# A fused attention, gated MLP and SoLU layer on one Trainium2 core: block 0's up products 512 tokens wide, x in the buffers of p

## Chip, core and metric

The kernel runs on one core of one Trainium2 chip. The metric is the device time of one execution in microseconds (us); the median of three runs of the kernel before is 970.23 us. Engines are called by the names of the profile: PE (TensorE, with PEld its weight loads), DVE (VectorE), ACT (ScalarE), POOL (GpSimd) and SP (SyncE, which here issues most DMAs). SPq is SP's sequencer.

## What is computed

Chunked attention with 8 memory keys a head, then two feed-forward layers on the 3072 tokens of 512 features that it yields:

```python
for c in range(24):                      # chunks of 32 tokens, keys c*32-16 .. c*32+40
    scores = scale * q_c @ concat(mem_k, k_ctx).T
    a = exp(scores - max); a = a / (sum(a) + 1e-9)
    out[c] = a @ concat(mem_v, v_ctx)
x = heads side by side                   # 3072 x 512
h = sigmoid(x @ w_gate) * (x @ w_val)    # 3072 x 1536
y = h @ w_out                            # 3072 x 512
z = y @ w_in                             # 3072 x 1024
s = z * softmax(z)
out = ((s - mean) / sqrt(var + 1e-6) * g_ln) @ w2_out
```

The weights come as 64-bit floats and are converted on the chip: a piece of 512 KB yields 128 x 512 values.

## The kernel before

The tokens are 24 tiles of 128. For tile t, the attention turns k and q on PE (`d_k`, `d_q`, four 128x128 transposes each, L446), takes the scores (`d_scores`, 64 small matmuls, L505), their maximum and exponential (`a_max`, `a_exp`, tile s), turns p (`d_p`), multiplies with v (`d_pv`), normalises (`d_norm`, tile xs) and turns the result (`d_x`), which ACT and DVE split into xh (`a_xhi`, L600) and xl (`a_xlo`, L604). The scores of tile t need the first keys of tile t + 1. p is the exponential in place: tile s holds both. The pool sp has two buffers of s and two of xs.

Four tiles are a block j of 512 tokens. For each of 12 groups m of 128 hidden features, `up` (L609 to L620) makes two products, one with the gate weights (gv = 0) and one with the val weights (gv = 1): 12 matmuls each, (wh, xh), (wh, xl) and (wl, xh) over four slices of the 512 features. `up_sig` (ACT) and `up_mul` (DVE) make g, which `g_store` writes to HBM; it is read again for `down`. In blocks 1 to 5 a matmul takes all 512 columns. In block 0, `steps_of` gives 256 tokens at a time: m = 0 to 10 for tiles 0 and 1, then m = 0 to 10 for tiles 2 and 3, then m = 11 for all four. A pair of products therefore needs only two tiles' x, but each weight passes PE twice.

A weight piece (m, gv) is loaded on SP's queue (`w_load`, L408), converted by ACT (`w_exp`, L204) and DVE (`w_bits`, L209 to L215), split by ACT (`w_hi`, L269) and POOL (`w_lo`, L220). The raw pieces share three buffers r and three larger spare places.

The order of all engines' work is made by the class `Plan`: each step has an engine, an assumed duration, steps it depends on, buffers it takes (`acq`, counted against the capacities given to `Plan`) and gives back (`rel`), and a due time, which is handed back from a step to those ahead of it. `order` puts the steps on their engines, the one due first among those that could start; no step is put more than AHEAD = 40 before it is due. The due times of the up products are a running clock from FIRST = 30, and x is due one unit before its block's first product that uses it, and LEAD earlier still in blocks 1 to 5. On the chip each engine executes its steps in the order so made, and waits with everything behind a step for that step.

Of the kernel before, what the change touches and what calls it, by code (L numbers as in the profile page):

```python
# [9 lines left out]
F32 = mybir.dt.float32  # L10
# [11 lines left out]
class Plan:  # L22
# [9 lines left out]
    def add(self, name, eng, dur, fn=None, deps=(), due=None, acq=(), rel=(), dma=(), table=None, prev=None, pad=0,  # L32
            slack=0):


        self.tasks[name] = dict(
            name=name, eng=eng, dur=dur, fn=fn, deps=list(deps), due=due, acq=list(acq), rel=list(rel),
            dma=dma, table=table, pad=pad, slack=slack, end=None, next=[], prev=prev if prev in self.tasks else None,
        )
# [84 lines left out]
def encoder_kernel(  # L124
# [16 lines left out]
    B, H, S, D = q.shape  # L141
# [10 lines left out]
    MF = FF // 128  # L152
# [75 lines left out]
    for m in range(MF):  # L228
        pieces.append((m, 0, w_out.bitcast(I32)[m * 128:(m + 1) * 128, :].unsqueeze(1)))
        if m < 2 * KM:  # L230
            kk, n = divmod(m, 2)
# [179 lines left out]
    at = ExitStack()  # L411
    raw = at.enter_context(tc.tile_pool(name="raw", bufs=2))
    tp = at.enter_context(tc.tile_pool(name="tp", bufs=2))
    ktp = at.enter_context(tc.tile_pool(name="ktp", bufs=3))
    sp = at.enter_context(tc.tile_pool(name="sp", bufs=2))
    sm = at.enter_context(tc.tile_pool(name="sm", bufs=2))

    R, QT, KT, VW, SS, PT, PS, RS, XS, X = ({} for _ in range(10))
# [39 lines left out]
    def d_load(nm, t):  # L458
        b, i = divmod(t, TB)
        R[nm, t] = raw.tile([128, H, D], F32, tag=nm, name=nm)  # L460
        src = dict(rk=k, rq=q)[nm][b, :, i * 128:(i + 1) * 128, :]
        nc.sync.dma_start(out=R[nm, t], in_=src.rearrange("h p d -> p h d"))
# [61 lines left out]
        nc.scalar.activation(out=SS[t], in_=SS[t], func=AF.Exp, scale=D ** -0.5)  # L524

    def a_sum(t):
        rs = RS[t] = sm.tile([128, H], F32, tag="rs", name="rs")
        nc.vector.tensor_reduce(out=rs, in_=SS[t], axis=AX.X, op=ALU.add)
        nc.vector.tensor_single_scalar(out=rs, in_=rs, scalar=1e-9, op=ALU.add)
        nc.vector.reciprocal(out=rs, in_=rs)  # L530
# [49 lines left out]
        PS[t, 2] = two_banks(PT[t], VW[t // 2][:, :, 4 * (t % 2):4 * (t % 2) + 4, :])  # L580

    def d_norm(t):
        XS[t] = sp.tile([128, H, D], F32, tag="xs", name="xs")
        rs = RS.pop(t).unsqueeze(2).to_broadcast([128, H, D]).rearrange("p (k x) d -> p x k d", x=2)
        out_ = XS[t].rearrange("p (k x) d -> p x k d", x=2)
        nc.vector.tensor_tensor(out=out_, in0=PS.pop((t, 2)), in1=rs, op=ALU.mult)
        SS.pop(t)

    def d_x(t):
        PS["dx", t] = d_turn("u0", XS.pop(t))  # L590
# [275 lines left out]
    def o_store(j, t):  # L866
# [2 lines left out]


    plan = Plan(dict(
        rk=2, rq=2, qT=2, pT=2, kT=3, vw=2, s=2, xs=2,
        a=2, P=1, Q=1, R=1, O=1, hs0=1, hs1=1, hu=1, y=1, ys=1, xh=2, xl=2, r=3, w=2, u0=2, u1=2, sg=2, g=2, gh=3, gl=3, so=2, nt=6, e=1, hi=2, lo=2, o=2,
        **{s: 1 for s in FIRST_TAGS},
    ))
    add = plan.add
    ACT, DVE, POOL, PE, SP = "act", "dve", "pool", "pe", "sp"
    HALVES, WIDE = 1, 1
    FIRST, RATE, LEAD, SLACK, EARLY, LATER = 30.0, 1.12, 20.0, 3.0, 140.0, 235.0

    ALONE = "c2", "nt", "gcol", "mhalf", "ident", "zero", "pb"

    def one(nm, t, eng, dur, fn, deps=(), **kw):
        add((nm, t), eng, dur, lambda: fn(t), deps=[d if isinstance(d, tuple) or d in ALONE else (d, t) for d in deps],
            prev=(nm, t - 1), **kw)
# [17 lines left out]
    for t in range(NTILE):  # L903
        n, u = divmod(t, 2)
        b, i = divmod(t, TB)
        early = t < 2
        one("rk", t, SP, 0.1, lambda t: d_load("rk", t), acq=[("rk", t)], dma=[1.456])
        one("dk", t, PE, 0.9 if early else 0.5, d_k, ["ident", "rk"], acq=[("u0", ("dk", t)), ("kT", t)], rel=[("rk", t)], slack=0 if t < 6 else SLACK)
        one("dkev", t, ACT, 1.35, d_kev, ["dk"], rel=[("u0", ("dk", t))])
        one("dhalo", t, POOL, 0.6, d_halo, ["dkev"] + ([("dhalo", t - 1)] if i else []))  # L910
        one("dkmem", t, POOL, 0.45, d_kmem, ["dkev", ("dmev", b)])
        one("rq", t, SP, 0.1, lambda t: d_load("rq", t), acq=[("rq", t)], dma=[1.456])
        one("dq", t, PE, 0.9 if early else 0.5, d_q, ["ident", "rq"], acq=[("u1", ("dq", t)), ("qT", t)], rel=[("rq", t)], slack=0 if t < 6 else SLACK)
        one("dqev", t, ACT, 0.58, d_qev, ["dq"], rel=[("u1", ("dq", t))])
        one("sw", t, PE, 1.3 if early else 0.75, d_scores,
            ["dqev", "dkmem", ("dhalo", t if i == TB - 1 else t + 1)],
            acq=[("a", t), ("s", t)], rel=[("qT", t), ("kT", t)], slack=0 if t < 6 else SLACK)
        one("max", t, DVE, 1.45, a_max, ["sw"], rel=[("a", t)])
        one("exp", t, ACT, 0.63, a_exp, ["max"], table="exp")
        one("sum", t, DVE, 1.25, a_sum, ["exp"])  # L920
        one("dp", t, PE, 0.9 if early else 0.5, d_p, ["exp"], acq=[("u1", ("dp", t)), ("pT", t)], slack=0 if t < 6 else SLACK)
        one("dpev", t, ACT, 0.58, d_pev, ["dp"], rel=[("u1", ("dp", t))])
        one("pv", t, PE, 1.3 if early else 0.75, d_pv, ["dpev", ("dv", n, 0), ("dv", n, 1), ("dvm", n)],
            acq=[("a", (t, 2)), ("xs", t)], rel=[("pT", t)] + ([("vw", n)] if u else []), slack=0 if t < 6 else SLACK)
        one("norm", t, DVE, 0.69, d_norm, ["pv", "sum"], rel=[("a", (t, 2)), ("s", t)])
        x = [("xh", t // 4), ("xl", t // 4)] if t % 4 == 0 else []
        one("dx", t, PE, 0.9 if early else 0.5, d_x, ["norm"], acq=[("u0", ("dx", t))] + x, rel=[("xs", t)], slack=0 if t < 6 else SLACK)
        one("xhi", t, ACT, 0.58, a_xhi, ["dx"] + ([] if t % 4 == 0 else [("xhi", t - 1)]))
        one("xlo", t, DVE, 0.69, a_xlo, ["xhi"], rel=[("u0", ("dx", t))])

# [1 line left out]

    def steps_of(j):

        if j >= HALVES:
            return [(m, (0, 512)) for m in range(MF)]
        wide = WIDE if j == 0 else 0
        return [(m, w) for w in ((0, 256), (256, 512)) for m in range(MF - wide)] + [
            (m, (0, 512)) for m in range(MF - wide, MF)
        ]  # L940

    for n, (m, gv, _) in enumerate(pieces):
        s, x = divmod(n - 3, 2)
# [3 lines left out]
        rel = [] if spare and not x else [key]  # L947
# [49 lines left out]
    clock = FIRST  # L997
    for j in range(NB):
        steps = steps_of(j)
        seen = set()  # L1000
        for s, (m, w) in enumerate(steps):
# [6 lines left out]
            for gv in range(2):  # L1008
# [6 lines left out]
                elif s == len(steps) - 1:  # L1015
# [3 lines left out]
                    rel=[("xh", j), ("xl", j)] if gv and s == len(steps) - 1 else [])  # L1019
            add(("sig", *key), ACT, 0.6 if full else 0.39, lambda k=key: up_sig(*k), deps=[("up", j, m, 0, w)],  # L1020
                acq=[("sg", key)], rel=[("u0", key)], table="sig", due=clock + 1)
# [8 lines left out]
    for m in range(MF):  # L1030
        one("gag", m, SP, 0.1, g_again, [("gst", 0, m, w) for y, w in steps_of(0) if y == m], acq=[("r", ("g", m))], dma=[0.73])
        add(("gmax", 0, m), DVE, 0.75, lambda m=m: g_max0(m), deps=[("gag", m)], rel=[("r", ("g", m))], due=EARLY + 4 + 8.0 * m)
# [12 lines left out]
    for j in range(NB):  # L1045
# [3 lines left out]
        for f in range(MF):  # L1049
            parts = [w for m, w in steps_of(j) if m == f]  # L1050
            tag, after = ("g", "sg")[f % 2], [("sig" if f % 2 else "mul", NB - 1, MF - 1, (0, 512))]
            if not f % 2:
                after.append(("gmax", NB - 1, MF - 1))
            if (j, f) in FIRST_G:
                tag, after = FIRST_G[j, f], ["c2"]
# [6 lines left out]
                acq=([(f"u{o % 2}", ("y", j, o)) for o in range(KM)] if j else [("a", ("y", o)) for o in range(2)]) if f == 0 else [], rel=[("gh", (j, f)), ("gl", (j, f))])  # L1062
        for o in range(KM):
            two("ycp", j, o, ACT, 0.62, y_copy, [("down", j, MF - 1)] + ([("ycp", j, 0)] if o else [("up", NB - 1, 11, 1, (0, 512))]),
                acq=[("y", j)] if o == 0 else [],
                rel=[(f"u{o % 2}", ("y", j, o))] if j else [("a", ("y", o // 2))] if o % 2 else [])
        if j == 0:
            add("pb", "mark", 0, open_pb, deps=[("ycp", 0, o) for o in range(KM)])
        for c in range(4):
            two("ysum", j, c, DVE, 0.72, y_sum, [("ycp", j, o) for o in range(KM)] + ([("ysum", j, c - 1)] if c else [("thi", x) for x in range(3, 7)] + [("tlo", x) for x in range(3, 7)]),  # L1070
                acq=[("ys", j)] if c == 0 else [])
            need = [("ycp", j, o) for o in range(KM)] + [("ysum", j, x) for x in ((), (), (0, 1), (2, 3))[c]]
            two("yhi", j, c, ACT, (1.15, 0.62, 1.15, 1.15)[c], y_hi, need + ([("yhi", j, 0)] if c else []),
                acq=[("xh", ("y", j)), ("xl", ("y", j))] if c == 0 else [])
            two("ylo", j, c, DVE, (1.35, 0.72, 1.35, 1.35)[c], y_lo, ["yhi"], rel=[("y", j), ("ys", j)] if c == 3 else [])
        for u in range(2):
            before = ("prod", j, 0, 3) if u else ("prod", j - 1, 1, 3)
            held = {3: [("hpart", j, u, "c22")], 2: [("hpart", j, u, "c1")], 7: [("hpart", j, u, "u2")], 4: [("hpart", j, u, "u3")]}
            for x in ORDER:
# [4 lines left out]
                    acq=[(bank, (j, u))] if x in (1, 6, 5) else [], rel=[("xh", ("y", j)), ("xl", ("y", j))] if u and x == 3 else [])  # L1084
# [3 lines left out]
            for part, (eng, need) in parts.items():  # L1088
                add(("hpart", j, u, part), eng, 0.62 if eng == ACT else 0.72, lambda j=j, u=u, p=part: h_part(j, u, p),
                    deps=[("prod", j, u, n) if isinstance(n, int) else ("hpart", j, u, n) for n in need] + ["w2done"],  # L1090
                    acq=[(f"hs{u}", (j, u)), ("hu", (j, u))] if part == "c1" else [],
                    rel={"c11": [("P", (j, u))], "c21": [("Q", (j, u))], "c12": [("R", (j, u)), ("hu", (j, u))]}.get(part, []))
        for t in range(4):
            u, x = TILE[t] % 2, TILE[t] // 2
# [3 lines left out]
                rel=[("e", (j, t, 1))] + ([(f"hs{u}", (j, u))] if x else []))  # L1098
# [10 lines left out]
                acq=[(OUT.get((j, t), "O"), (j, t))], rel=[("nt", (j, t))])  # L1109
# [3 lines left out]
    for p in range(2 * NB):  # L1113
        j, u = divmod(p, 2)
        m = [("prod", j, u, x) for x in ORDER]
# [51 lines left out]
```

## Time and profile before

| | |
|---|---|
| median of three runs | 970.23 us (969.41 to 971.39) |
| the profiled execution | 970.33 us |
| its span | 968.6 us |
| mean granted clock of TensorE | 0.989 |
| PE busy | 924.2 us (95%) |
| DVE busy | 613.7 us |
| ACT busy | 434.7 us |
| POOL busy | 91.3 us |

All times within the execution are counted from the start of the span. The busy time of PE counts matmuls, whose records overlap one another: the distance between the starts of two of them tells more of the pace than their durations. [...]

### The profile page before, as it was taken

The numbers are of one execution on the slowest core, as the hardware profiler recorded it, in microseconds if no ns is written. First come the engines' busy times: TensorE is split into PE (matmuls) and PEld (weight loads), VectorE is DVE, ScalarE is ACT, GpSimd is POOL, SyncE is SP. The second block draws the span as 40 slices with busy tenths as digits, with TensorE's granted clock in tenths as the row PEclk, the third lists the DMA queues.
The fourth block names the chain that finished last, engine by engine and source line by source line (L and its number), as shares of the span: only waits on it lengthen the run. The fifth ranks groups of instructions, "written<-read, shape, count | busy, mean of one in ns | idle before, by whom it ended". The sixth has DMA issues, their size and how long they took to land.

```text
span 968.6 us, 18485 instructions
## 1 busy us (share of the span) xinstructions
PE 924.2 (95%) x7408; PEld 614.5 (63%) x7408; DVE 613.7 (63%) x1156; ACT 434.7 (45%) x705; POOL 91.3 (9%) x154
## 2 busy tenths in 40 slices
PE   3777989999999999999999999999999999999998
PEld 2667888878888888788788644444444444444443
DVE  5787553377657757747745336786765764867581
ACT  4566542145245435326514243644544633645452
POOL 3343200001000000000003300000000000000000
PEclk9988989999999999999999999999999999999999
DMA  8999895367648746732575232434244144242323
GB/s 203 234 242 205 203 205 169 103 177 169 192 134 173 193 128 172 180 146 99 165 256 189 76 98 66 120 86 100 66 98 109 55 109 98 77 98 44 77 65 98
DMA packets 202949, 132.68 MB, mean 137 GB/s; under 512 B 153136, under 2 KB 170288, under 8 KB 202672
## 3 DMA queue, kind: packets, MB, share of 16 engines
q1 hardware_dynamic: 192624, 105.29, 43.9%
q10 hardware_dynamic: 10240, 26.22, 8.9%
q8 instruction: 58, 0.95, 0.4%
q14 instruction: 27, 0.22, 0.1%
HBM read 86.38 MB, written 33.03 MB: 123 GB/s over the span
## 4 chain that ended last, share of the span: by engine, by line
PE 89%; DMA 4%; ACT 3%; DVE 2%; SPq 2%; issue 1%; ACTq 0%; DVEq 0%
PE u L619 39%; PE y L711 19%; PE ps L856 13%; PE Q L764 5%; PE tr L446 4%; PE ps L505 3%; PE R L764 3%; PE P L764 3%; DMA r<-in_moe_w_gate_dram 1%; DMA r<-in_moe_w_val_dram 1%; SPq L569 1%; DMA vw<-mv 1%; DMA rq<-in_q_dram 1%; DVE w L210 0%; ACT L524 0%
## 5 line engine op out<-in xcount | busy, mean ns | idle before, releaser
L619 PE MATMUL u<-xh,wa 128*128 128x512 f32 (+1 forms) x1328 | 386.7, 371 | 3.7 <-ACT wa L269 1.4
L619 PEld LDWEIGHTS u<-xh,wa 128*128 128x128 f32 x1328 | 245.2, 194 | 44.5 <-ACT wa L269 1.7
L619 PE MATMUL u<-xl,wa 128*128 128x512 f32 (+1 forms) x664 | 243.7, 367 | 0.6 <-DVE xl L604 0.5
L711 PE MATMUL y<-gh,pl 128*128 128x512 f16 x576 | 176.0, 379 | 0.0
L711 PEld LDWEIGHTS <-pl 128*128 128x128 f16 x864 | 84.5, 98 | 102.0 <-issue 0.5
L619 PEld LDWEIGHTS u<-xl,wa 128*128 128x128 f32 x664 | 129.1, 194 | 19.3 <-DVE xl L604 1.5
L630 DVE TENSOR_TENSOR g<-sg,u 128x512 f32<-128x512 f32 (+1 forms) x83 | 51.1, 615 | 127.7 <-PE u L619 56.3
L856 PE MATMUL ps<-wo,nt 128*128 128x512 f16 x576 | 127.6, 379 | 0.8 <-ACT o L863 0.8
L625 ACT ACTIVATE sg<-u 128x512 f32<-128x512 f32 (+1 forms) x83 | 44.9, 542 | 160.1 <-PE u L619 117.1
L711 PE MATMUL y<-gl,pl 128*128 128x512 f16 x288 | 109.2, 379 | 0.0
L432 ACT ACTIVATE gh<-gi,gm 128x512 f16<-128x512 f32 x72 | 51.5, 719 | 127.1 <-PE y L711 121.1
L856 PEld LDWEIGHTS <-nt 128*128 128x128 f16 x576 | 56.2, 98 | 69.2 <-issue 1.3
L222 DVE SCALAR_TENSOR_TENSOR gl<-gi,gm,gh 128x512 f16<-128x512 f32 x72 | 53.7, 750 | 66.3 <-ACT gh L432 66.0
L764 PEld LDWEIGHTS <-yh 128*128 128x128 f16 x336 | 32.9, 98 | 39.7
L824 POOL TENSOR_TENSOR ls<-ls,mhalf 128x1 f32<-128x1 f32 x24 | 14.6, 611 | 370.8 <-DVE ls L820 332.4
L204 ACT ACTIVATE w<-r 128x512 f32<-128x512 f32 x46 | 30.7, 669 | 27.1 <-DMA r<-in_moe_w_gate_dram 8.6
L764 PE MATMUL Q<-pl,yh 128*128 128x512 f16 x144 | 42.8, 379 | 0.0
L281 DVE TENSOR_REDUCE gm<-g 128x1 f32<-128x512 f32 x60 | 41.0, 684 | 1.8
L785 DVE TENSOR_TENSOR pl<-Q,pl 128x512 f32<-128x512 f32 x36 | 24.8, 688 | 25.7 <-PE Q L764 25.3
L220 POOL TENSOR_TENSOR wa<-w,wa 128x512 fp32r<-128x512 f32 x24 | 34.1, 1425 | 59.1 <-ACT wa L269 57.4
L213 DVE SCALAR_TENSOR_TENSOR w<-r,w 128x512 int32<-128x512 int32 x46 | 38.6, 839 | 1.6
L797 ACT ACTIVATE e<-pl,ls,few 128x1024 f32<-128x1024 f32 x24 | 29.7, 1237 | 18.0 <-DVE ls L806 10.0
(126 smaller groups left out, 1106.5 us busy)
## 6 DMA issues: line engine op xcount, KB each, us to landing
gi<-gd SPq DMA_DIRECT2D x72, 256.0 KB
gd<-g SPq DMA_DIRECT2D x61, 256.0 KB
r<-in_moe_w_out_dram ACTq DMA_DIRECT2D x28, 512.0 KB
vw<-in_v_dram SPq DMA_DIRECT2D x64, 98.0 KB
rk<-in_k_dram SPq DMA_DIRECT2D x24, 256.0 KB
rq<-in_q_dram SPq DMA_DIRECT2D x24, 256.0 KB
out_dram<-o SPq DMA_DIRECT2D x24, 256.0 KB
wd<-r SPq DMA_DIRECT2D x20, 256.0 KB
```

Source lines behind the costliest of these rows:

```text
L213: nc.vector.scalar_tensor_tensor(out=d, in0=hi, scalar=-(2 ** 31), in1=d, op0=ALU.bitwise_and, op1=ALU.bitwise_or)
L220: nc.gpsimd.tensor_tensor(out=dst, in0=x, in1=hi, op=ALU.subtract)
L222: nc.vector.scalar_tensor_tensor(out=dst, in0=x, scalar=s, in1=hi, op0=ALU.mult, op1=ALU.subtract)
L281: nc.vector.tensor_reduce(out=dst, in_=a, axis=AX.X, op=ALU.max, apply_absolute_value=True)
L432: nc.scalar.activation(out=dst, in_=x, func=AF.Copy, scale=s)
L446: nc.tensor.transpose(pv[:, kk, :], src[:, 2 * kk:2 * kk + 2, :], ident[0:rows, 0:rows])
L619: nc.tensor.matmul(u, lhsT=a, rhs=c[:, kk, w[0]:w[1]], start=(n == 0), stop=(n == 3 * KM - 1))
L625: nc.scalar.activation(out=sg, in_=U.pop((j, m, 0, w)), func=AF.Sigmoid)
L630: nc.vector.tensor_tensor(out=g, in0=U.pop((j, m, "s", w)), in1=U.pop((j, m, 1, w)), op=ALU.mult)
L711: nc.tensor.matmul(y, lhsT=a, rhs=c, start=(f == 0 and n == 0), stop=(f == MF - 1 and n == 2))
L764: nc.tensor.matmul(ps, lhsT=yc[a][:, c, kk, u * 128:(u + 1) * 128], rhs=t[:, hl, kk, :], start=(first and n == 0), stop=(n == 5), skip_gro ...
L856: nc.tensor.matmul(ps, lhsT=nt[:, a, kk, :], rhs=C["wo2"][:, c, kk, :], start=(n == 0), stop=(n == 3 * K2 - 1))
```

## The change

`steps_of` gives (m, (0, 512)) for block 0 as for the others, and the constants HALVES and WIDE go. The normalised product of tile t is written into the tile that held its scores and p (`d_norm`); the tag xs is gone, the pool has four buffers of s instead of two and two, and the row sums have four buffers. In the plan the place s is given back when x has been turned (`dx`), and xs is no longer asked for. LEAD is 30 instead of 20.

```diff
-    sp = at.enter_context(tc.tile_pool(name="sp", bufs=2))
+    sp = at.enter_context(tc.tile_pool(name="sp", bufs=4))
...
-        rs = RS[t] = sm.tile([128, H], F32, tag="rs", name="rs")
+        rs = RS[t] = sm.tile([128, H], F32, tag="rs", name="rs", bufs=4)
...
     def d_norm(t):
-        XS[t] = sp.tile([128, H, D], F32, tag="xs", name="xs")
+        XS[t] = SS.pop(t)
...
-        SS.pop(t)
...
-        rk=2, rq=2, qT=2, pT=2, kT=3, vw=2, s=2, xs=2,
+        rk=2, rq=2, qT=2, pT=2, kT=3, vw=2, s=4,
...
-    HALVES, WIDE = 1, 1
-    FIRST, RATE, LEAD, SLACK, EARLY, LATER = 30.0, 1.12, 20.0, 3.0, 140.0, 235.0
+    FIRST, RATE, LEAD, SLACK, EARLY, LATER = 30.0, 1.12, 30.0, 3.0, 140.0, 235.0
...
         one("pv", t, PE, 1.3 if early else 0.75, d_pv, ["dpev", ("dv", n, 0), ("dv", n, 1), ("dvm", n)],
-            acq=[("a", (t, 2)), ("xs", t)], rel=[("pT", t)] + ([("vw", n)] if u else []), slack=0 if t < 6 else SLACK)
-        one("norm", t, DVE, 0.69, d_norm, ["pv", "sum"], rel=[("a", (t, 2)), ("s", t)])
+            acq=[("a", (t, 2))], rel=[("pT", t)] + ([("vw", n)] if u else []), slack=0 if t < 6 else SLACK)
+        one("norm", t, DVE, 0.69, d_norm, ["pv", "sum"], rel=[("a", (t, 2))])
...
-        one("dx", t, PE, 0.9 if early else 0.5, d_x, ["norm"], acq=[("u0", ("dx", t))] + x, rel=[("xs", t)], slack=0 if t < 6 else SLACK)
+        one("dx", t, PE, 0.9 if early else 0.5, d_x, ["norm"], acq=[("u0", ("dx", t))] + x, rel=[("s", t)], slack=0 if t < 6 else SLACK)
...
     def steps_of(j):
 
-        if j >= HALVES:
-            return [(m, (0, 512)) for m in range(MF)]
-        wide = WIDE if j == 0 else 0
-        return [(m, w) for w in ((0, 256), (256, 512)) for m in range(MF - wide)] + [
-            (m, (0, 512)) for m in range(MF - wide, MF)
-        ]
+        return [(m, (0, 512)) for m in range(MF)]
```

## Rows read from the trace of the kernel before

**Rows 1.** The page: PE's and the other engines' busy time, granted clock, DMA packets.

```profile
PE 924.2 (95%) x7408; PEld 614.5 (63%) x7408; DVE 613.7 (63%) x1156; ACT 434.7 (45%) x705; POOL 91.3 (9%) x154
...
PEclk9988989999999999999999999999999999999999
...
DMA packets 202949, 132.68 MB, mean 137 GB/s; under 512 B 153136, under 2 KB 170288, under 8 KB 202672
```

**Rows 2.** Busy us (instructions) by stretch: PE, PEld, DVE, ACT, POOL; PEclk, DMA share, GB/s.

```profile
0.00:36.40 36.40, 14.56 (x296) 10.97 (x297) 22.90 (x39) 17.65 (x36) 11.18 (x22) 1.00 0.98 219
36.40:50.00 13.60, 13.60 (x97) 13.35 (x98) 10.15 (x16) 7.21 (x13) 5.69 (x4) 1.00 1.14 211
50.00:92.00 42.00, 30.86 (x562) 28.12 (x561) 33.56 (x55) 27.99 (x58) 18.20 (x23) 0.87 1.04 230
92.00:118.00 26.00, 25.62 (x316) 24.92 (x316) 16.68 (x32) 16.24 (x28) 7.54 (x10) 0.94 0.82 200
118.00:129.10 11.10, 6.86 (x164) 6.00 (x162) 7.68 (x16) 6.13 (x13) 0.62 (x3) 0.85 1.17 194
129.10:152.00 22.90, 22.90 (x351) 22.42 (x350) 11.20 (x22) 9.79 (x18) 0.62 (x3) 0.92 0.84 220
...
157.50:543.80 386.30, 383.98 (x3664) 314.21 (x3663) 240.08 (x457) 153.14 (x254) 31.15 (x63) 1.00 0.56 161
```

**Rows 3.** Chain of waits in order of time: start us, us, what.

```profile
81.46 7.08 DMA r<-in_moe_w_gate_dram
```

**Rows 4.** Timeline of SP's queue: start us, us until the last is issued, what, count.

```profile
0.72 0.46 SPq L408 DMA_DIRECT2D r<-in_moe_w_gate_dram  x1
...
30.90 1.35 SPq L408 DMA_DIRECT2D r<-in_moe_w_val_dram  x1
32.34 4.64 SPq L462 DMA_DIRECT2D rk<-in_k_dram  x2
...
41.26 6.74 SPq L560 DMA_DIRECT2D vw<-in_v_dram  x8
```

**Rows 5.** Timeline of DVE: xl of tiles 0 and 1 (first row) and of tile 3.

```profile
35.57 1.28 DVE L604 TENSOR_TENSOR xl<-tr,xh 128x512 fp32r<-128x512 f32 x2
...
92.08 0.68 DVE L604 TENSOR_TENSOR xl<-tr,xh 128x512 fp32r<-128x512 f32 x1
```

**Rows 6.** Timeline of PE: xl matmuls of up, every third matmul of a product.

```profile
37.72 0.41 PE L619 MATMUL u<-xl,wa 128*128 128x256 f32 x1
...
38.36 0.41 PE L619 MATMUL u<-xl,wa 128*128 128x256 f32 x1
...
42.88 0.28 PE L619 MATMUL u<-xl,wa 128*128 128x256 f32 x1
...
43.24 0.28 PE L619 MATMUL u<-xl,wa 128*128 128x256 f32 x1
...
153.46 0.39 PE L619 MATMUL u<-xl,wa 128*128 128x512 f32 x1
...
154.14 0.39 PE L619 MATMUL u<-xl,wa 128*128 128x512 f32 x1
```

**Rows 7.** Groups of instructions with shapes kept apart: count | busy us, mean ns | idle before.

```profile
L619 PE MATMUL u<-xh,wa 128*128 128x256 f32 x352 | 74.1, 306 | 2.3 <-ACT wa L269 1.4 <-ACT kT L474 0.7 <-DVE g L630 0.2
```

**Rows 8.** Timeline of PE: attention steps that follow one another, 70 to 73 us.

```profile
71.14 0.86 PE L505 MATMUL ps<-kT,qT 64*32 64x64 f32 x64
71.93 0.66 PE L446 MATMUL tr<-ident,rk 128*128 128x128 f32 x4
72.52 0.86 PE L505 MATMUL ps<-vw,pT 64*32 64x64 f32 x64
```

**Rows 9.** Timeline of PE: up products that begin or go on after a wait.

```profile
51.66 0.39 PE L619 MATMUL u<-xh,wa 128*128 128x256 f32 x1 [0.67 <-ACT kT L474]
...
90.81 0.86 PE L505 MATMUL ps<-kT,qT 64*32 64x64 f32 x64 [2.69 <-ACT qT L494]
91.72 0.58 PE L619 MATMUL u<-xh,wa 128*128 128x256 f32 x1
```

## Prediction

> **What bounds the kernel now.** I read the page's parts 1 and 2 first. TensorE (PE) is busy for 924.2 of 968.6 us, so 44.4 us of idle time are all that better overlap can win, plus what a lower clock costs; PEclk says that the clock is lower only in the first eighth of the span [rows 1]. Then the busy time by stretches. From 157.5 to 543.8 us, where up blocks 1 to 5 run, PE is busy for 383.98 of 386.30 us at clock 1.00: whatever reaches that stretch earlier leaves it earlier. Ahead of it lie the losses: 21.8 us idle before the first up product at 36.4 us, 11.1 between 50 and 92, 4.2 between 118 and 129, with a granted clock of 0.85 to 0.94 from 50 to 152 [rows 2]. In the same table the DMA share is near 1 until 92 us while VectorE (DVE) is busy for 33.56 and ScalarE (ACT) for 27.99 of the 42 us from 50 to 92, so that early part is set by loads, and by engines that work in order behind a load.
>
> The chain of waits in order of time shows which loads: from 50 us on they are single pieces of the weights, one of them waited for during 7.08 us [rows 3]. A weight piece that is late holds ACT at its first conversion, and the copies of the attention tiles stand behind it in ACT's order. The queue of SyncE (SP) shows why the first products could start at 36.4 us: by then twelve of the 24 gate and val pieces had been issued among the loads of tiles 0 and 1, and tiles 2 and 3 (k, q, v) only from 32.34 to 48.00 us [rows 4]. Their x is finished at 92.8 us, against 36.9 for tiles 0 and 1 [rows 5]. So before, the first half of block 0 (256 tokens) runs at the pace of the weights, and the second half must wait until 92 us.
>
> **The change, part by part.** My sum is made against the profiled execution, 970.33 us, whose span is 968.6; the median shown is 970.23, a tenth lower.
>
> *Later start.* All four tiles' x is now needed ahead of the first product. Their due time in the planner is the same as that of tiles 0 and 1, while piece n of the weights, whose due times were crowded by two short products for each m, now has two products of 2.73 us in between: the loads of tiles 2 and 3 go ahead of nearly all weights. In the trace these loads held SP's queue for 15.7 us (32.34 to 48.00), behind weights already in flight [rows 4]. If nothing gave way to them, the start would move by that, to 52. If all twelve early pieces gave way, their own 9.3 us on the queue (the sum of the twelve issues, of which the first and the last stand in rows 4) come off and the start moves by 6.4, to 43. But m = 0 must be there, and conversions run beside the attention; I take the middle, +11.0, a start at 47.4 us. What it lacks in cover: PE has nothing else to do until then but attention.
>
> The trace bears on one more thing: the first 36.4 us moved 219 GB/s with weights and attention loads mixed [rows 2], and 153136 of the 202949 packets of the span are under 512 B [rows 1]. [...]
>
> *Attention of tiles 2 and 3.* It is moved into that wait, off the later stretch. A warm tile costs PE four turns of 0.59 us and two products (scores, p times v) of 0.79: the scores begin at 71.14, the next turn at 71.93, the next product at 72.52 [rows 8]. That is 3.9 us for one, and -7.9 us for both.
>
> *Products.* 528 matmuls of 256 columns (352 with xh, the others with xl) become 264 of 512 [rows 7]. Between two xl matmuls, which are three matmuls apart, lie 0.36 us at full clock with 256 columns (42.88 to 43.24), and 0.68 with 512 (153.46 to 154.14) [rows 6]: 0.120 and 0.227 each, so 528 x 0.120 = 63.4 against 264 x 0.227 = 59.9, -3.5 us. Sigmoids and multiplications halve in number too (22 to 11), as do block 0's stores of g; both lie beside PE, so I cost them at nothing, and they are worth something only where DVE or ACT holds the chain.
>
> *Stalls after the start.* Before: 11.1 + 0.4 + 4.2 = 15.7 us idle between 36.4 and 152 [rows 2]. Also, five times the products restart with 0.213 us for a matmul instead of 0.120 (37.72 to 38.36 for three), for some 3.5 us each; the first restart follows the wait at the start [rows 6], the fourth, at 91.72, a wait of 2.69 us [rows 9]: 5 x 3.5 x (1 - 0.120/0.213) = 7.6 us. Together 23.3. Now each arriving m gives PE 5.44 us of work instead of 2.88. Before, half products kept up with the weights: five m's (m = 4 to m = 8) took from 51.66 to 91.72 us [rows 9], 8 us for each. Now 5.44, plus the attention of tiles 4 to 7, 4 x 3.9 = 15.6 us over some seven m's, makes 7.7 us of work for each m: nearly the pace of the loads. So most gaps are covered by products already possible. But the waits where an attention step on PE stands behind ACT, which is held by a weight load, remain in kind, and the tiles of block 1 are pulled forward by the larger LEAD (30 for 20) into the same time. The bounds are nothing gained and 18 us gained (idle and slow clock of a single stretch such as 118 to 129 left over); I take half, -11.0.
>
> *Four shared buffers.* x of tile t is written over its p; the scores of tile t + 4 now wait for the turning of x(t), where those of t + 2 waited for its normalisation. It is the same memory, no instruction is added, and the wait is two tiles further off. DVE's first reduction of tile t + 4 is what would stand there, with DVE's queue behind it; the turning of x(t) is issued long before, so it costs nothing unless PE itself is late, and then PE's lateness is already counted.
>
> *Later blocks.* LEAD moves their attention 10 us earlier. 2.3 us idle are left in the whole of 157.5 to 543.8 [rows 2], so this is between +2 and -2; I take 0.
>
> Sum: 11.0 - 7.9 - 3.5 - 11.0 = -11.4, and 970.33 - 11.4 = 958.9 us. I forecast 959. What is late next at the end of block 0 is PE itself.
>
> **The rivals.**
> First rival: the stalls stay. In-order waits of attention behind weight loads are 15.7 us whatever the products' width, and the clock falls as often: 11.0 - 7.9 - 3.5 = -0.4, 970 us, no change. For it: waits as at 51.66 and 90.81 us are for a copy of the attention on ACT [rows 9], and wide products do not shorten them. Against it: PE's order then had only short products between these steps.
>
> Second rival, slower: tiles 2 and 3 get stuck in the weights' conversions. ACT and DVE take up weight pieces in an order made with faster loads than the trace shows; a piece that lands 7 us late [rows 3] holds every copy and exponential behind it, and tile 3's x holds the first product. Each us of start costs one. With half the stalls left the change breaks even at 47.4 + 11.4 = 58.8 us; two such held pieces more than I counted, and one more stall, put the start near 66 and the time at 977. For it: tiles 2 and 3 took from 32 to 92 us before. Against it: they were then placed behind the weights.
>
> Third rival, larger gain: all twelve pieces give way (a start at 43, +6.4) and 18 us of stalls go: 6.4 - 7.9 - 3.5 - 18 = -23, 947 us.
>
> That the change doesn't do what it says has a small place: were the tiles' loads still queued behind the weights, it would be the second rival.
>
> **How the numbers follow.** Forecast (950 to 967) 0.53; stalls stay (967 to 973) 0.15; slower by a late start (973 to 985) 0.17; larger gain (940 to 950) 0.15. The range 945 to 975 leaves out a part of the last two. About 0.2%, 1.9 us, is what a measurement of this kernel can tell from no change. Faster by more: the forecast, the larger gain and a part of the first rival, 0.73. Within it: 0.10. Slower: the second rival, 0.17.
>
> **What would show it.** The first up product near 47 us, and not past 58. The last xl of tiles 0 to 3 just ahead of it, with at most some six weight pieces issued before the v loads of tiles 2 and 3. No 256-column matmul; a step of 0.227 us at full clock in block 0. Block 0 at an end near 146 us instead of 157.5, with idle time between the start and that end below 10 us and fewer restarts at 0.427 us for a matmul. PE as dense from there to the end of the up products, which then end near 532 instead of 543.8. I am wrong if the start is late (second rival), if idle time merely moves (first), or if blocks 1 to 5 show new gaps.

## The result, and the profile after

The changed kernel takes 957.58 us (median of 4 runs, 954.59 to 959.73), the kernel before 970.81 beside it; the ratio is 0.9862, with a 95% interval of 0.9831 to 0.9892. It is faster by 13.2 us where 11.4 were forecast. The profiled execution took 954.59 us with a span of 952.8, so the traces differ by 15.8 us; the ledger (the account of where the time went) below goes by them.

First the page of the kernel after, whose line of busy times answers [rows 1].

```profile
PE 916.1 (96%) x7144; PEld 595.3 (62%) x7144; DVE 615.8 (65%) x1145; ACT 422.7 (44%) x686; POOL 88.6 (9%) x154
```

There are 264 matmuls fewer; PE is busy for 8.1 us less, and idle for 36.7 us instead of 44.4: 8.1 + 7.7 = 15.8. The busy time by stretches tells where, with the columns of [rows 2] (us, busy PE, PEld, DVE, ACT, POOL, then PEclk, DMA share, GB/s). The first two rows have the limits of rows of before; the others are cut at what happens in the kernel after.

```profile
0.00:36.40 36.40, 19.16 (x481) 15.04 (x482) 13.55 (x29) 14.30 (x35) 3.94 (x21) 0.90 1.00 161
36.40:50.00 13.60, 8.87 (x134) 6.86 (x119) 12.42 (x18) 7.59 (x12) 4.63 (x4) 0.64 1.11 330
...
0.00:45.83 45.83, 23.85 (x586) 18.59 (x586) 22.12 (x42) 19.78 (x44) 6.48 (x23) 0.85 1.02 200
...
45.83:70.00 24.17, 24.17 (x103) 19.83 (x104) 21.82 (x29) 13.96 (x27) 11.11 (x13) 0.92 0.96 205
70.00:110.00 40.00, 34.26 (x586) 27.32 (x585) 32.91 (x56) 26.75 (x47) 12.89 (x15) 0.91 0.94 219
110.00:130.00 20.00, 20.00 (x153) 16.40 (x152) 17.23 (x24) 9.25 (x15) 7.79 (x6) 1.00 1.10 222
130.00:150.00 20.00, 16.69 (x82) 13.85 (x82) 10.25 (x16) 5.99 (x15) 3.44 (x8) 1.00 0.87 266
150.00:528.30 378.30, 377.30 (x3698) 309.67 (x3697) 242.02 (x463) 151.03 (x253) 30.59 (x63) 1.00 0.58 167
528.30:952.80 424.50, 419.85 (x1944) 189.68 (x1942) 269.42 (x519) 195.94 (x286) 16.25 (x28) 1.00 0.35 87
```

The first product begins at 43.43 us, waits for tile 3's xl and goes on from 45.83 without a gap; until then PE is idle for 21.98 us, as before (21.84). From there to 150 us it is idle for 5.74 + 3.31 = 9.05 us, where 15.7 stood before. The products of blocks 1 to 5 end at 528.3 instead of 543.8, with 1.0 us of idle time in them instead of 2.3.

Next the timeline of SyncE's queue, which answers [rows 4] (start us, us until the last is issued, what, count).

```profile
10.67 5.91 SPq L569 DMA_DIRECT2D mv<-in_mem_v_dram  x8
...
18.73 4.64 SPq L560 DMA_DIRECT2D vw<-in_v_dram  x8
...
24.30 0.40 SPq L408 DMA_DIRECT2D r<-in_moe_w_gate_dram  x1
24.74 4.88 SPq L560 DMA_DIRECT2D vw<-in_v_dram  x4
...
30.91 0.40 SPq L408 DMA_DIRECT2D r<-in_moe_w_val_dram  x1
```

DVE's timeline has the xl of tile 3, which answers the last of [rows 5].

```profile
45.09 0.68 DVE L604 TENSOR_TENSOR xl<-tr,xh 128x512 fp32r<-128x512 f32 x1
```

The v loads of tiles 2 and 3 (half of the eight and all of the four) are issued by 29.6 us, where before they were issued from 41.26 us on, and a single weight piece goes ahead of their last part. Tile 3's x is finished at 45.8 us instead of 92.8.

PE's timeline shows what is left of the stalls; it answers [rows 6] and [rows 9] (start us, us, what, in brackets the idle time before and its releaser).

```profile
43.43 0.79 PE L619 MATMUL u<-xh,wa 128*128 128x512 f32 x1 [0.68 <-ACT xh L600]
45.83 0.79 PE L619 MATMUL u<-xl,wa 128*128 128x512 f32 x1 [1.61 <-DVE xl L604]
...
47.27 0.63 PE L619 MATMUL u<-xl,wa 128*128 128x512 f32 x1
...
48.55 0.63 PE L619 MATMUL u<-xl,wa 128*128 128x512 f32 x1
...
50.39 0.39 PE L619 MATMUL u<-xl,wa 128*128 128x512 f32 x1
...
51.08 0.39 PE L619 MATMUL u<-xl,wa 128*128 128x512 f32 x1
...
93.56 1.11 PE L446 MATMUL tr<-ident,s 128*128 128x128 f32 x4 [3.01 <-ACT qT L494]
...
146.63 0.66 PE L446 MATMUL tr<-ident,rq 128*128 128x128 f32 x4 [3.31 <-DVE g L630]
```

xl matmuls three apart stand 1.28 us apart after the start (47.27 to 48.55, 0.427 for a matmul) and 0.69 at full clock (50.39 to 51.08, 0.23). This slow beginning occurs twice, from 45.8 to 49.7 and from 94.3 to 97.4 us, where before it occurred five times: some 7.0 us at 0.427, of which 3.3 are lost to the pace, instead of 7.6. The granted clock in these two stretches is 0.52 (0.50 from 47.27 to 48.55 us, and 1.00 from 50.39 to 51.08):

```profile
45.83:49.70 3.87, 3.87 (x10) 3.06 (x11) 3.56 (x6) 1.82 (x3) 1.80 (x2) 0.52 1.19 297
94.30:97.40 3.10, 3.10 (x10) 2.48 (x9) 2.14 (x4) 3.09 (x5) 0.93 (x2) 0.52 0.28 73
```

In the kernel before the granted clock doesn't tell it all: it is 1.00 from 36.40 to 50.00 us [rows 2], although the first slow beginning (37.72 to 38.36 for three matmuls) lies there [rows 6]. The distance between matmuls shows that one, and it is what this account goes by.

The chain of waits, as in [rows 3], shows what the rest of the idle time hangs on.

```profile
85.16 6.61 DMA r<-in_moe_w_val_dram
91.86 0.66 ACT w L204
...
93.02 0.49 ACT qT L494
...
134.25 6.25 DMA r<-in_moe_w_out_dram
...
141.24 4.03 DMA r<-gd
```

The wait at 93 us has the pattern of before: a weight piece lands late, ACT converts it, the copy qT of an attention tile stands behind that in ACT's order, and PE waits for the copy. The wait at 143 us is of another kind: DVE's reductions wait for pieces of the out weights and for g read again (gd), and the multiplication that PE needs stands behind them.

### The profile page after: what moved, and what is told of

It reads as the page before. It is cut to its first block, busy times and chain, and to the rows that moved or that the text cites. A ratio compares the mean times of both kernels' runs of the same rounds, so it can differ in the third digit from the quotient of the medians.

```text
span 952.8 us, 17894 instructions
## 1 busy us (share of the span) xinstructions
PE 916.1 (96%) x7144; PEld 595.3 (62%) x7144; DVE 615.8 (65%) x1145; ACT 422.7 (44%) x686; POOL 88.6 (9%) x154
## 4 chain that ended last, share of the span: by engine, by line
PE 86%; DMA 6%; DVE 3%; SPq 1%; issue 1%; ACT 1%; POOL 0%; ACTq 0%; DVEq 0%
PE u L619 36%; PE y L711 20%; PE ps L856 13%; PE Q L764 5%; PE tr L446 4%; PE R L764 3%; PE P L764 3%; PE ps L505 3%; DMA vw<-in_v_dram 2%; DMA r<-in_moe_w_val_dram 1%; SPq L560 1%; DVE w L210 1%; DMA rq<-in_q_dram 1%; DVE w L209 1%; DMA r<-in_moe_w_out_dram 1%
## 5 line engine op out<-in xcount | busy, mean ns | idle before, releaser
L619 PE MATMUL u<-xh,wa 128*128 128x512 f32 x1152 | 370.6, 397 | 1.3 <-ACT xh L600 0.7
L619 PEld LDWEIGHTS u<-xh,wa 128*128 128x128 f32 x1152 | 218.1, 189 | 47.5 <-ACT xh L600 0.9
L619 PE MATMUL u<-xl,wa 128*128 128x512 f32 x576 | 225.9, 392 | 1.6 <-DVE xl L604 1.6
L619 PEld LDWEIGHTS u<-xl,wa 128*128 128x128 f32 x576 | 109.2, 190 | 23.7 <-DVE xl L604 2.1
L630 DVE TENSOR_TENSOR g<-sg,u 128x512 f32<-128x512 f32 x72 | 49.3, 685 | 93.2 <-PE u L619 57.8
L625 ACT ACTIVATE sg<-u 128x512 f32<-128x512 f32 x72 | 43.0, 597 | 123.3 <-PE u L619 86.6
L446 PE MATMUL tr<-ident,s 128*128 128x128 f32 x192 | 31.0, 293 | 8.0 <-ACT qT L494 3.0
```

Source lines behind the costliest of these rows:

```text
L446: nc.tensor.transpose(pv[:, kk, :], src[:, 2 * kk:2 * kk + 2, :], ident[0:rows, 0:rows])
L619: nc.tensor.matmul(u, lhsT=a, rhs=c[:, kk, w[0]:w[1]], start=(n == 0), stop=(n == 3 * KM - 1))
L625: nc.scalar.activation(out=sg, in_=U.pop((j, m, 0, w)), func=AF.Sigmoid)
L630: nc.vector.tensor_tensor(out=g, in0=U.pop((j, m, "s", w)), in1=U.pop((j, m, 1, w)), op=ALU.mult)
```

## Experiments

Every kernel was compared with the kernel before on the same chip, whose medians there were 970.0 to 971.2 us. A diff is against the kernel after unless it says otherwise. Where a step of the plan changes, the planner makes the whole order anew; where only what a step issues changes, the order of steps stays. That difference turned out to matter.

### The three parts, one by one

Width alone: the kernel before, with block 0's steps 512 wide.

```diff
-    HALVES, WIDE = 1, 1
+    HALVES, WIDE = 0, 0
```

> Only the width of block 0's products is changed: 512 tokens at once, with two buffers of s and two of xs and LEAD 20 as before. Theory (the width carries the gain, since each weight pair then brings 5.44 us of work): 957 to 961 us, first up product between 45 and 49 us. Rival (four tiles can only be ready early because four buffers let their scores run ahead): the first product comes past 52 us and the time is 965 us or more.

Measured: 964.42 us, 0.9935 (0.9913 to 0.9958).

The buffers alone: the kernel after with block 0's steps and the LEAD of before.

```diff
-    FIRST, RATE, LEAD, SLACK, EARLY, LATER = 30.0, 1.12, 30.0, 3.0, 140.0, 235.0
+    FIRST, RATE, LEAD, SLACK, EARLY, LATER = 30.0, 1.12, 20.0, 3.0, 140.0, 235.0
...
+        if j == 0:
+            return [(m, w) for w in ((0, 256), (256, 512)) for m in range(MF - 1)] + [(MF - 1, (0, 512))]
```

> Only the buffers are changed: x over p, four buffers, halves of 256 tokens and LEAD 20 as before. Theory: no wait in the trace of before was for a buffer of s or xs, so 969 to 972 us. Rival (buffers are what held tiles 2 and 3 back): 5 us or more faster, with x of tile 3 finished well before 92 us.

Measured: 970.56 us, 1.0003 (0.9990 to 1.0017).

LEAD alone: the kernel before with LEAD 30.

```diff
-    FIRST, RATE, LEAD, SLACK, EARLY, LATER = 30.0, 1.12, 20.0, 3.0, 140.0, 235.0
+    FIRST, RATE, LEAD, SLACK, EARLY, LATER = 30.0, 1.12, 30.0, 3.0, 140.0, 235.0
```

> Only LEAD is changed, from 20 to 30. Theory: PE is dense in blocks 1 to 5 and the waits of the first 130 us are not for due times, so 968 to 973 us. Rival (tiles 4 to 7 pulled ahead end the wait from 118 to 129 us): 964 to 967 us.

Measured: 970.97 us, 1.0012 (0.9997 to 1.0027).

Width and buffers without LEAD: the kernel after with LEAD 20.

```diff
-    FIRST, RATE, LEAD, SLACK, EARLY, LATER = 30.0, 1.12, 30.0, 3.0, 140.0, 235.0
+    FIRST, RATE, LEAD, SLACK, EARLY, LATER = 30.0, 1.12, 20.0, 3.0, 140.0, 235.0
```

> The changed kernel with LEAD 20 again. Theory: within 2 us of the changed kernel, 956 to 960 us, either sign. Rival (LEAD 30 is what has tiles 4 to 7 ready by the end of block 0): 962 us or more, with new idle time at the border of blocks 0 and 1.

Measured: 961.61 us, 0.9904 (0.9880 to 0.9928).

What follows: the wide steps bring 5.6 us alone; with them the buffers bring 2.8 more (964.42 to 961.61) and LEAD another 4.0 (to 957.58). Without them neither brings anything. That the two together are worth something with the wide steps is clear (0.9935 against 0.9862, whose intervals lie apart). How they share it is not as sure: the interval of LEAD 20 overlaps both. DVE's timeline of width alone, with tile 3's xl, and then its stretches show why.

```profile
52.70 0.68 DVE L604 TENSOR_TENSOR xl<-tr,xh 128x512 fp32r<-128x512 f32 x1
```

```profile
0.00:53.44 53.44, 26.48 (x589) 20.77 (x589) 21.32 (x44) 19.75 (x45) 6.53 (x23) 0.67 1.02 207
53.44:150.00 96.56, 92.45 (x898) 74.73 (x899) 75.50 (x115) 57.12 (x103) 38.09 (x40) 0.95 0.90 201
150.00:539.00 389.00, 381.91 (x3716) 311.80 (x3716) 248.27 (x468) 154.82 (x258) 30.99 (x63) 1.00 0.58 168
```

With two buffers of s and two of xs, tile 3 is ready 7.6 us later than in the kernel after. PE is idle for 26.96 us before the start and for 7.1 us in blocks 1 to 5; between them for only 4.1. With four shared buffers (LEAD 20) the same xl starts at 45.68 us, and what is left stands in blocks 1 to 5:

```profile
160.00:450.00 290.00, 285.13 (x3283) 232.59 (x3282) 191.89 (x390) 117.64 (x211) 14.36 (x56) 1.00 0.57 154
```

PE is idle for 4.9 us there, in short waits for DVE's and ACT's results, none longer than 1.2 us. In the kernel after, the same stretch is:

```profile
160.00:450.00 290.00, 289.00 (x3309) 236.76 (x3308) 194.85 (x393) 121.89 (x215) 13.95 (x56) 1.00 0.57 154
```

So LEAD is what keeps blocks 1 to 5 dense once block 0 ends early. Between these two executions, whose spans are 957.1 and 952.8, LEAD's 4.3 us are 3.9 less of idle time there and 3.2 less of PE's busy time (919.3 and 916.1), less what the time before is idle for the longer. Of the 3.2 us, 1.9 lie ahead of the first product (25.73 us busy until 46.42, against 23.85 until 45.83); why PE is slower there with LEAD 20 was not found.

### Is it the width of a matmul?

First each pair of halves as two steps of the plan, one behind the other, for each m.

```diff
+        if j == 0:
+            return [(m, w) for m in range(MF - 1) for w in ((0, 256), (256, 512))] + [(MF - 1, (0, 512))]
         return [(m, (0, 512)) for m in range(MF)]
```

> The changed kernel with block 0's products 256 tokens wide again, but both halves of each m one behind the other, so that all four tiles are needed at the start and each weight pair brings the same work. Theory (the gaps close because the work of an m comes together, and the width itself is worth 3.5 us): 960 to 963 us, first product near 46 us, idle time of PE after it as in the changed kernel. Rival (fewer, longer instructions are the gain: half the sigmoids, multiplications and stores free ACT, DVE and SP): 966 us or more.

Measured: 973.81 us, 1.0025 (1.0015 to 1.0035). Three products of the first two tiles run from 43.47 us on; the second halves begin at 51.83 us, 6.0 us later than the products of the kernel after, and from there the stretches are:

```profile
51.83:150.00 98.17, 83.57 (x1090) 80.06 (x1091) 71.24 (x121) 53.81 (x107) 33.35 (x39) 0.91 0.90 202
150.00:540.00 390.00, 383.12 (x3716) 313.64 (x3715) 244.86 (x466) 148.68 (x253) 23.76 (x61) 1.00 0.58 166
```

PE is idle for 14.6 us instead of 9.05, then for 6.9 instead of 1.0; the last weight piece is issued at 138.29 us instead of 123.51, and the longest wait of PE from 51 to 150 us (us, times, longest) is:

```profile
PE tr L446 <- DVE g L630: 6.3, 1, 6.3
```

That looks like a price of 16 us for narrow products. But this kernel has twice the sigmoids, multiplications and stores of block 0, and an order made anew, so it can't say which. The next one holds the order of steps: each product of block 0 is issued as two runs of 12 matmuls of 256 columns, and nothing else changes.

```diff
+        for lo in ((0, 256) if j == 0 else (0,)):
+            hi = lo + 256 if j == 0 else 512
...
-                nc.tensor.matmul(u, lhsT=a, rhs=c[:, kk, w[0]:w[1]], start=(n == 0), stop=(n == 3 * KM - 1))
+                    nc.tensor.matmul(u[:, lo:hi], lhsT=a, rhs=c[:, kk, lo:hi], start=(n == 0), stop=(n == 3 * KM - 1),
...
```

> The changed kernel with its planned order untouched; only each product of block 0 is issued as two of 256 columns one behind the other (same sigmoids, multiplications and stores). Theory (the width alone is worth what PE's pace says): 3.5 us slower than the changed kernel, 960 to 962 us. Rival (the loss of 16 us with the halves as steps of their own was the width): 966 us or more.

The kernel after was run again beside it, so that the two stand on one chip:

> The changed kernel itself, beside the three that follow. 956 to 959 us by every theory.

Measured: 955.14 us with the split (0.9840, 0.9819 to 0.9860) and 955.63 without (0.9844, 0.9828 to 0.9861). The stretches of the split kernel, to be read against the rows with the same limits of the kernel after:

```profile
0.00:45.83 45.83, 25.85 (x597) 20.87 (x597) 21.75 (x40) 19.18 (x43) 6.53 (x23) 0.84 1.00 195
45.83:70.00 24.17, 23.43 (x179) 23.43 (x180) 22.60 (x30) 14.00 (x27) 10.79 (x12) 0.89 0.91 204
70.00:110.00 40.00, 35.85 (x671) 33.37 (x671) 32.83 (x56) 26.83 (x47) 13.38 (x15) 0.91 0.98 222
110.00:130.00 20.00, 20.00 (x226) 19.77 (x225) 18.04 (x26) 9.95 (x16) 7.79 (x6) 1.00 1.06 229
130.00:150.00 20.00, 19.64 (x129) 17.74 (x128) 10.36 (x16) 6.48 (x16) 3.46 (x8) 1.00 0.82 256
```

From 45.83 to 150 us PE is busy for 98.91 us instead of 95.12, 3.8 more (by the pace of [rows 6], all narrow products cost 576 x 0.120 - 288 x 0.227 = 3.7), and the end hardly moves. DVE begins the last multiplication of block 0 at 141.55 us; the kernel after has 141.13 and 141.23 in its two profiles. First the kernel after, then the split one:

```profile
141.13 0.68 DVE L630 TENSOR_TENSOR g<-sg,u 128x512 f32<-128x512 f32 x1
```

```profile
141.55 0.69 DVE L634 TENSOR_TENSOR g<-sg,u 128x512 f32<-128x512 f32 x1 [0.80 <-PE u L622]
```

The narrow matmuls fill time in which PE would have waited, and not only after the start: the first twelve need only two tiles' x, run from 43.42 us on, and PE is busy for 2.0 us more before 45.83. So this compares the narrow matmuls with that small head start, and both together cost nothing that these runs can measure (four runs of each, 953.5 to 959.6 and 954.8 to 959.2 us).

What pays instead is not isolated. That all four tiles' x is there first and that each m's work for 512 tokens follows at once is not enough as an account: the kernel of pairs has the second, and the first 6.0 us later, and is 16 us slower. What it also lacks is the halved number of sigmoids, multiplications and stores, and the order that the planner made for wide steps. No kernel here changes the number of these operations and holds the order.

### x early, the order of halves kept

The kernel after with block 0's steps as before (all first halves, then all second halves), but with x of all four tiles due ahead of the first product.

```diff
+        if j == 0:
+            return [(m, w) for w in ((0, 256), (256, 512)) for m in range(MF - 1)] + [(MF - 1, (0, 512))]
...
-                    plan.tasks["xlo", t]["due"] = clock - 1 - (LEAD if j else 0)
+                    plan.tasks["xlo", t]["due"] = clock - 1 - LEAD if j else FIRST - 1
```

> The changed kernel with block 0 in the order of before (256 tokens of m = 0 to 10, then the other 256), but x of all four tiles due at the start. Theory (a late start with only 2.88 us of work for each arriving m leaves the gaps and pays the delay): 968 to 980 us, PE idle again between 50 and 95 us. Rival (having the loads of tiles 2 and 3 ahead of the weights is the gain, in whatever order the products stand): 958 to 963 us.

Measured: 977.13 us, 1.0064 (1.0048 to 1.0080).

```profile
54.60:100.00 45.40, 37.63 (x389) 36.22 (x390) 35.64 (x58) 28.82 (x57) 18.22 (x23) 0.88 0.91 211
100.00:150.00 50.00, 43.73 (x696) 40.98 (x696) 30.82 (x54) 23.78 (x46) 10.99 (x13) 1.00 0.90 214
```

PE pays a start at 54.6 us, 8.8 later than in the kernel after, and still has 7.8 and 6.3 us of stalls. Early x without the new order of products is a loss here. The weights' due times are crowded again in this kernel, so the start is later than was meant; whether the stalls after it hang on that too was not tested.

### What the start costs

Eight small copies of the memory values (`d_vexp`) hold SyncE's queue for 5.91 us (SyncE's timeline of the kernel after), ahead of tile 3's q and of the v loads of tiles 2 and 3. In the first kernel they go to ACT's queue, ahead of all else, and the plan, which no longer sees them, is made anew.

```diff
-                nc.sync.dma_start(out=MV[b][x, :, kk], in_=src[x, :, kk:kk + 1, :].to_broadcast([NM, 8, D]))
+                (nc.sync if b else nc.scalar).dma_start(out=MV[b][x, :, kk], in_=src[x, :, kk:kk + 1, :].to_broadcast([NM, 8, D]))
...
+    d_vexp(0)
     for part in plan.order():
```

> The changed kernel with the first eight small copies of mem_v issued from ACT's queue at the very start, not from SP's in the middle of the loads. They hold SP's queue for 5.9 us ahead of the loads of tiles 2 and 3. Theory (each us of start is worth one, since PE has nothing else to do until then): the first product 3 to 6 us earlier, near 41 us, and the time 952 to 955 us. Rival (the weights set the pace, so that an earlier start only waits later): first product earlier, time 957 to 959 us.

Measured: 957.78 us, 0.9864 (0.9842 to 0.9886), as the kernel after. Tile 3's xl begins at 40.31 us, 4.8 us earlier, and by 150 us PE has been busy for 4.5 us longer. From there on the lead is lost: the profiled execution's span is 954.6 us, against 952.8. Two stretches show a part of it:

```profile
150.00:300.00 150.00, 148.55 (x1687) 122.14 (x1686) 94.05 (x189) 62.05 (x117) 7.36 (x33) 1.00 0.70 170
300.00:450.00 150.00, 147.01 (x1654) 120.14 (x1653) 104.68 (x211) 59.68 (x104) 6.72 (x26) 0.99 0.51 149
```

PE is idle for 4.4 us where the kernel after has 1.0. The view of PE's waits from 150 to 530 us (us, times, longest) names the most of this idle time, a wait for ACT's exponential that the kernel after doesn't have there:

```profile
PE tr L446 <- ACT s L524: 3.5, 2, 2.1
```

To hold the order, the second kernel leaves the plan alone and issues the copies on ACT's queue ahead of it.

```diff
-    def d_vexp(b):
+    def d_vexp(b, queue=None):
+        if b == 0 and queue is None:
+            return
...
-                nc.sync.dma_start(out=MV[b][x, :, kk], in_=src[x, :, kk:kk + 1, :].to_broadcast([NM, 8, D]))
+                (queue or nc.sync).dma_start(out=MV[b][x, :, kk], in_=src[x, :, kk:kk + 1, :].to_broadcast([NM, 8, D]))
...
+    d_vexp(0, nc.scalar)
     for part in plan.order():
```

> The changed kernel with its planned order untouched; only the first eight copies of mem_v are issued from ACT's queue ahead of everything, so SP's queue is 5.9 us shorter ahead of tile 3's loads. Theory (each us of start is worth one, and what took it back in the run before was the re-made order): x of tile 3 at 40 to 42 us and 952 to 955 us. Rival (the loads of the weights set the pace after the start): x of tile 3 as early, but 956 to 959 us.

Measured: 956.77 us, 0.9851 (0.9832 to 0.9869). It does not do what it was for: tile 3's xl begins at 47.16 us, 2.1 us later, not earlier (in the profiled execution, the slowest of five). ACT's timeline shows the price of the other queue:

```profile
0.73 7.23 ACTq L571 DMA_DIRECT2D mv<-in_mem_v_dram  x8
7.99 1.28 ACT L474 ACT_TABLE_LOAD   x1 [7.99 <-DMA mv<-in_mem_v_dram]
```

ACT issues the eight copies for 7.23 us before it does anything else; its first copy kT begins at 9.28 us, where the kernel after has 5.28, and PE waits 4.0 us for it. On SyncE's queue the eight v loads of the first fence (four of them of tiles 2 and 3) begin only 2.0 us earlier, though 5.91 us of copies are gone ahead of them, and they end 0.6 us earlier, at 22.8 us, since the 4.64 us that they took are now 6.05:

```profile
16.77 6.05 SPq L560 DMA_DIRECT2D vw<-in_v_dram  x8
```

The kernel ahead of this one has the same delay on ACT (kT at 9.48 us) and x early all the same, so there it seems to be the order made anew that brought it forward. What an earlier start would bring in the order of the kernel after stays open. A later start can be had: the third kernel issues each of the eight copies twice, the second time to a place that nobody reads.

```diff
+    MV2 = dr.tile([2, NM, KM, 8, D], F32, name="mvx")
...
+                if b == 0:
+                    nc.sync.dma_start(out=MV2[x, :, kk], in_=src[x, :, kk:kk + 1, :].to_broadcast([NM, 8, D]))
```

> The changed kernel with its planned order untouched; the eight copies of mem_v are issued twice on SP's queue (the second into a place that nobody reads), so the start is delayed. Theory: x of tile 3 some 5 us later, near 50 us, and 961 to 964 us. Rival (the weights, also delayed on that queue, or the loads after them set the pace): the time moves by less than half of what the start moves.

Measured: 963.54 us, 0.9933 (0.9914 to 0.9952), 7.9 us above the kernel after beside it. A copy more took 0.63 us of the queue (SyncE's timeline, first fence), and tile 3's xl is 5.5 us late (DVE's, second):

```profile
13.36 0.63 SPq L572 DMA_DIRECT2D mvx<-in_mem_v_dram  x1
```

```profile
50.64 0.68 DVE L607 TENSOR_TENSOR xl<-tr,xh 128x512 fp32r<-128x512 f32 x1
```

The profiled execution is 4.2 us longer in its span than the first one after (957.0 and 952.8) and the end of block 0 comes 4.0 us later (145.14). A us of delay cost about one here: 4 to 8 us for 5.5. It is the delay of all that stands behind the copies, not of the start alone: the second weight piece, issued at 30.91 us in the kernel after, is issued at 36.37 here.

### The wait at the end of block 0

PE waits for 3.3 us at 143 us, behind DVE's reductions for the out weights and for g read again, which wait for their loads. This kernel makes that work due 50 later.

```diff
-    FIRST, RATE, LEAD, SLACK, EARLY, LATER = 30.0, 1.12, 30.0, 3.0, 140.0, 235.0
+    FIRST, RATE, LEAD, SLACK, EARLY, LATER = 30.0, 1.12, 30.0, 3.0, 190.0, 285.0
```

> The changed kernel with EARLY and LATER 50 later (190 and 285), so that the reductions of re-read g and of w2_out come later in DVE's order. Theory (the wait of PE of 3.3 us at 143 us for a multiplication stands behind those reductions, which wait for their loads): that wait goes, 953 to 956 us. Rival (another step takes its place, or the work moved collides later): 957 us or more.

Measured: 968.42 us, 0.9974 (0.9958 to 0.9990).

```profile
130.00:150.00 20.00, 20.00 (x98) 16.75 (x97) 5.61 (x9) 6.48 (x16) 3.01 (x8) 1.00 0.32 93
150.00:537.70 387.70, 378.88 (x3679) 308.90 (x3677) 251.10 (x470) 148.11 (x250) 30.21 (x63) 0.99 0.59 169
...
250.00:300.00 50.00, 47.40 (x669) 37.74 (x658) 39.78 (x84) 24.59 (x44) 3.58 (x16) 0.93 0.70 176
```

The wait is gone, and 8.8 us of idle time stand in blocks 1 to 5 instead of 1.0. That what was moved collides there with the attention of the later tiles is likely, but not shown. And idle time is the smaller part of the loss. In the whole span (966.7 us, against 952.8) PE is idle for 39.9 us instead of 36.7, but busy for 926.8 instead of 916.1, at a mean granted clock of 0.977 instead of 0.987; between 250 and 300 us it is 0.93, where the kernel after has 1.00. No kernel was found that beats the kernel after by more than its own runs differ.

## Why the prediction was right, and where not

**Later start and attention.** Forecast: a start at 47.4 us, +11.0, and -7.9 for two tiles' attention moved into it, +3.1 together. The products run from 45.83 us, +9.4, and PE was busy for 23.85 us until then instead of 14.56, so the pair came to +0.1. Of "at most some six weight pieces" one went ahead of the last v loads. The rates of the loads have no term of their own in the sum, and the 15.7 us from which I started were measured on loads of this kind. The rate is higher in the stretches where a smaller part of the packets is under 512 B, though no run separates their size from all else: with the attention loads first, the first 36.4 us moved 161 GB/s at a DMA share of 1.00 (17352 of 18594 packets under 512 B), and the next 13.6 us 330 GB/s at 1.11 (1882 of 5797). Before, it was 219 GB/s (9612 of 14965) and 211 (7791 of 8668) [rows 2]. One reading of the queue was off: k of tile 2 had been issued at 13.00 us, so of the two k loads at 32.34 us only one was for tiles 2 and 3, the other for tile 4.

**Stalls.** Forecast -11.0 of 23.3. Idle time fell from 15.7 to 9.05 us, -6.7, and the loss to the slow beginnings from 7.6 to 3.3, -4.3: -11.0. The idle time is below 10 us and the restarts are two instead of five, as written. That it is -11.0 to the tenth is luck: "half" was of bounds of 0 and 18, which is 9 (and 961 for the sum), and half of the 23.3 is 11.7. The split kernel bears out a part of the reason given: work added to PE in this stretch vanishes in its waits. That more work for each m is what closed the gaps is not shown, as the kernel of pairs has it too and is idle for 14.6 us. The kind of wait that was to remain does remain (93.56 us, for ACT's qT behind a weight piece).

**Products.** Forecast -3.5 us. PE's busy time fell by 8.1, which leaves about that much beside the 4.3 of the slow beginnings. As a part of the sum it is the step that failed: it holds only where PE sets the pace, and the split kernel, with 3.8 us put back after the start, takes the same time. The ledger of the two traces hides this, since less busy time and more waiting stand in different lines. So the sum was right by a little luck: without the 3.5 it would have forecast 962.

**Four buffers and LEAD.** Both were costed at nothing, LEAD at 0 within 2 us. Alone they are worth nothing. With wide steps the buffers bring some 2.8 us: four tiles' attention now runs ahead of the first product, and with four places of s tile 3's xl begins 7.0 us earlier (45.68 against 52.70); I had looked only at the wait that they add, not at the one that they take away. LEAD brings some 4.0, twice its bound: I read the 2.3 us idle of blocks 1 to 5 before as all that there was to win, while an earlier end of block 0 opens new waits there (7.1 us with width alone, 4.9 with the buffers), and LEAD closes them.

**Block 0's end and after.** Forecast near 146 us and 532; measured 141.8 and 528.3. "What is late next at the end of block 0 is PE itself" was wrong: PE ends its matmuls of block 0 near 139 us (a product of block 1, 12 x 0.227 us, follows until the turns at 141.85), and at 143.3 waits 3.3 us for DVE, which waits for loads of the out weights and of g. Moving that work was worse.

**The sum of the two traces.** +0.1 for start and attention, -11.0 stalls, -3.5 products (by the pace, as forecast), -1.3 less idle time in blocks 1 to 5, +0.2 in the last stage: -15.5 of -15.8. The rivals: stalls that stay (970) are refuted in the kernel after, and a start that is late did not come, but both exist close by, in the kernel with x early and the old order of halves (977).

## What to carry to other kernels

Price a faster instruction at nothing in a stretch whose chain of waits runs through loads and another engine: here 3.8 us more of matmuls vanished in the waits. An edit that looks free by itself (a buffer more, an earlier due time) is to be priced against the kernel as the other edits leave it. Where a planner orders all engines anew at each change, compare with kernels in which the order is held: narrow matmuls seemed to cost 16 us with a new order (and twice the work around them), and cost nothing that the runs can measure with the order held (955.14 us against 955.63).

## What the runs showed of the chip

- One small copy of the memory values, from HBM to HBM, took 0.63 us of SyncE's queue in the kernel that issues each twice; in the kernel after, the eight stood for 5.91 us in front of loads that the first products waited for. The same eight v loads took 4.64 us of the queue in one kernel and 6.05 in another.
- Eight copies issued on ACT's queue ahead of its work took 7.23 us; ACT's first operation began at 7.99 instead of 0.72 us, and its first copy kT at 9.28 instead of 5.28.
- With one and the same order of instructions, eight executions of the kernel after range over 5.1 us (954.6 to 959.7). It is no peculiarity of this kernel: twenty of the kernel before on one chip range over 4.7 (968.8 to 973.5). What makes the difference was not found.
